# A retention layer and a Strassen feed-forward on one core: one pool of eight PSUM banks, q loaded in permuted 1 KB rows, and wider feed-forward sums

## The chip, the core and the metric

The kernel runs on one core of a Trainium2 chip. A core has TensorE (PE, the matrix multiplications), VectorE (DVE), ScalarE (ACT), GpSimd (POOL) and SyncE (SP), which here issues transfers; each engine runs its own list of instructions in order, and semaphores hold an instruction until those on other engines that it depends on are done. DMA engines move data between HBM and SBUF; PSUM holds the results of TensorE in banks of 2 KB for each of 128 partitions, here 512 numbers of fp32. The metric is the time of one execution on the device in microseconds (us), the median of several.

## What is computed

Eight sequences of 576 positions with eight heads of width 64 go through a retention layer (attention without softmax, with a decay for each head), and the result through a feed-forward layer with a squared ReLU:

```python
scores = (q @ k.transpose(0, 1, 3, 2)) / sqrt(64)
gamma  = 1.0 - 2.0 ** (-5.0 - arange(8))            # one for each head
ret    = scores * where(i >= j, gamma ** (i - j), 0)
attn   = ret @ v                                    # [8, 8, 576, 64]
x      = attn.transpose(0, 2, 1, 3).reshape(4608, 512)
h      = x @ w_in                                   # 512 -> 2048
out    = maximum(h, 0) ** 2 @ w_out                 # 2048 -> 512
```

Inputs and output are fp32; the kernel multiplies in fp16 and accumulates in fp32.

## The kernel before

**Units and groups.** A unit is 128 positions: 32 "full" units (a stretch of 128 positions of one sequence) and 4 "tail" units (the last 64 positions of two sequences). Two units form a group, 18 in all. The first eight units are "paired" and take another path, with their transposes on TensorE; the other 28 are what most of the change touches.

**Retention of a group.** k, q and v of a unit are loaded by SyncE (`add_load`, L284), cast to fp16 by POOL (L359, `fk` and `fq` in `add_unit`) and, for v, scaled with the decay (L371, `fv`). A DMA transpose (L384) gives kqT, heads and positions turned round. All multiplications of the retention are done by `quad` (L345): four matmuls of 64x64 side by side on TensorE's array. They come in four kinds: scores psc (`emit_scores`, L602), which DVE masks into rT (L682, `after_scores`); state sums psS (`emit_sums`, L613), which DVE turns into the running states Rm, stmp and R (`after_sums`); the share of the earlier state, "out1" (L648), and the rest, "out2" (L653), which add up in psO. DVE scales psO with the decay into xT (L736, `after_outs`), the left side of the feed-forward.

**Joined clusters.** For groups g from 7 to 16 the quads of two groups are joined (`add_ret`, L751): f1 is out1 of g and the scores of g+1; f2 is the sums of g+1 and out2 of g. Each is one unbroken stretch on TensorE. f2 needs the masked scores and the casts of both groups.

**Feed-forward of a group** (`add_ff`, L836). Eight blocks: 8 matmuls of 128x256 into one PSUM bank ph (L859), a ReLU on ACT (L867) into rl, and a square into gT, on ACT (L877) for seven blocks and on DVE (L879) for one (five of eight on DVE in the last two groups). The second product, from group 2 on, is a 2x2 Strassen scheme in Winograd's form (`add_strassen`, L915): seven products p1 to p7 of 8 matmuls each (L951), whose left sides are either parts of gT or four sums of parts, S1 to S4, made by DVE (L928, tile gS), and whose right sides are parts of w_out or differences of them, wT (L811). DVE makes each of the four sums in two halves of 512 columns, eight operations per group. Products collect in banks po, copied out by ACT (L964) and added by DVE (L974) into the output tile o.

**PSUM.** Four single banks (tag `ff`) rotate between ph, po and a few others. The retention has two pairs of banks: `prS` for psc, `prO` for psO; psS takes one of the two. A pair comes free as a whole.

**The order.** `Schedule` (L16 to L93) is a list planner that runs while the program is built: each task has an engine, a key (lower is preferred), a length, tasks that it follows and resources with counts (`ff=4`, `prS=1`, `prO=1`, `rT=4`, ...). It runs the tasks through an event model and writes them out in the order in which they start there; the engines then run that order as it stands, whatever the true times are. A length or a count changed in the planner can therefore move instructions of every engine. In a joined cluster of the kernel before, TensorE's order is: 40 matmuls of ph, 16 of po, 12 ph, 4 po, 4 ph, 12 po, 4 ph, 8 po; then f1 (16 groups of out1 quads, 32 of scores); 4 ph, 16 po; then f2 (32 of sums, 48 of out2).

Of the kernel before, what the change touches and what calls it, by code (L numbers as in the profile page):

```python
# [103 lines left out]
def kernel(  # L104
# [48 lines left out]
    ps_ff = ctx.enter_context(tc.tile_pool(name="ps_ff", bufs=4, space=bass.MemoryType.PSUM))  # L153
    ps_ret = ctx.enter_context(tc.tile_pool(name="ps_ret", bufs=1, space=bass.MemoryType.PSUM))
# [42 lines left out]
    heads = [(4 * n + 2 * a + b, n, a, b) for n in range(2) for a in range(2) for b in range(2)]  # L197
    lncol = const.tile([P, NP], FP32, name="lncol")
    lnrow_R = const.tile([P, NP], FP32, name="lnrow_R")
    for h, n, a, b in heads:  # L200
        nc.vector.memset(lncol[64 * b:64 * b + 64, 2 * n + a:2 * n + a + 1], lng[h])
        nc.vector.memset(lnrow_R[64 * a:64 * a + 64, 2 * n + b:2 * n + b + 1], lng[h])

    mask = const.tile([P, 64], FP32, name="mask")
    nc.gpsimd.memset(mask, 1.0)
    for c in range(2):
        nc.gpsimd.affine_select(out=mask[c * 64:(c + 1) * 64], in_=mask[c * 64:(c + 1) * 64],  # L207
                                compare_op=ALU.is_ge, fill=0.0, base=0, pattern=[[1, 64]], channel_multiplier=-1)
# [9 lines left out]
    for hp in range(NP):  # L218
        nc.scalar.activation(out=gam_f[:, hp, :], in_=iota_f, func=ACTF.Exp, scale=lncol[:, hp:hp + 1])
    gam = {"full": gam_f.rearrange("p n (c i) -> p c n i", c=2),  # L220
           "tail": gam_f[:, :, 0:64].rearrange("p n (c i) -> p c n i", c=1).to_broadcast([P, 2, NP, 64])}
# [7 lines left out]
    SPREAD = 0.1  # L229
    SQ_LATE = (1, 4, 6)  # L230
# [4 lines left out]
    SHARED = ()  # L235
    FIRST = ["k0", "q0", "v0", "k2", "q2", "v2", "w0", "w1", "w2", "w3", "w4", "w5", "w6", "w7", "k4", "q4", "v4", "k6", "q6", "v6"]
    sched = Schedule(dict(ff=4, prS=1, prO=1, g=3, ld=5, wst=4, kq=7, v16=7, rT=4, x=3, rl=3, o=4, p1=2, u2=2, u4=2,
# [6 lines left out]
    warm_ps = []  # L244

# [17 lines left out]
    def make_tail_pool():  # L263
        iota_pt = tile_of["iota_pt"] = const.tile([P, 1], FP32, name="iota_pt")
        nc.gpsimd.tensor_copy(out=iota_pt[0:64], in_=iota_p[0:64])
        nc.gpsimd.tensor_scalar(out=iota_pt[64:128], in0=iota_p[64:128], scalar1=-64.0, scalar2=None, op0=ALU.add)
    tail_pool = add_gated("POOL", 4, "v", 2.2, make_tail_pool)
# [14 lines left out]
    def add_load(u):  # L282
        kind, b, c = units[u]
        for n, (name, src) in enumerate((("k", k), ("q", q), ("v", v))):  # L284
            def fn(name=name, src=src):
                x = ld.tile([P, H, D], FP32, name=f"{name}32", tag=f"{name}32")
                tile_of[name + "32", u] = x
                if kind == "full":
                    nc.sync.dma_start(out=x, in_=src[b, :, c * P:(c + 1) * P, :].rearrange("h p d -> p h d"))
                else:  # L290
                    for i in range(2):
                        nc.sync.dma_start(out=x[i * 64:(i + 1) * 64],
                                          in_=src[b + i, :, 512:576, :].rearrange("h p d -> p h d"))
            loaded[name, u] = dma_task(0, 1.2 if loaded else 2.1, fn, acq=("ld",) if n == 0 else ())
# [58 lines left out]
    def add_unit(u, base):  # L353
# [4 lines left out]
        def sorted_cast(op, out_, in_):  # L358
            op(out=out_.rearrange("p (n b a d) -> p n b a d", n=2, b=2, a=2),  # L359
               in_=in_.rearrange("p (n a b) d -> p n b a d", n=2, a=2))  # L360
# [5 lines left out]
        def fq():  # L366
            sorted_cast(nc.gpsimd.tensor_copy, tile_of["kq", u][:, 1], tile_of["q32", u])
# [19 lines left out]
    def add_unit_pair(u, base):  # L387
# [4 lines left out]
        for i, name in enumerate("kqv"):  # L392
            xs[name] = []
            for e in range(2):
# [3 lines left out]
                def fc(name=name, e=e, eng=eng):  # L398
# [8 lines left out]
                    else:  # L407
                        engines[eng](out=t.rearrange("p (n b a d) -> p n b a d", n=2, b=2, a=2),
                                     in_=x.rearrange("p (n a b) d -> p n b a d", n=2, a=2))
# [42 lines left out]
    def add_ret_pair(g):  # L452
# [7 lines left out]
        for e in range(2):  # L460
            tag = "prS" if e == 0 else "prO"

            def fs(e=e, tag=tag):
                ps = rT["ps", e] = ps_ret.tile([P, 2, 512], FP32, name="psc", tag=tag)
                rT[e] = cast.tile([P, 2, NP, P], FP16, name="rx", tag="kq16")
                for hp in range(NP):
                    for a, s in ((0, 0), (1, 1), (0, 1), (1, 0)):
                        quad(ps[half(s), a, hp * P:(hp + 1) * P], kqT(s)[half(a), hp, half(e)], kqT(s)[half(a), NP + hp, :],
                             a, s)
            t = add("PE", base + 3 + e, 0.4, fs, deps=T["kqT", u] + T["kqT", u + 1], acq=(tag, "kq"))  # L470
            ms = []
            for a in range(2):
                def fm(e=e, a=a):
                    nc.vector.tensor_tensor(
                        out=rT[e][:, a], in0=rT["ps", e][:, a].rearrange("p (n i) -> p n i", i=P),
                        in1=mask2[:, e].rearrange("p (o e) i -> p o (e i)", o=1).to_broadcast([P, NP, P]), op=ALU.mult)
                def fc(e=e):
                    nc.scalar.copy(out=rT[e][:, 1], in_=rT["ps", e][:, 1].rearrange("p (n i) -> p n i", i=P))

                def fp(e=e):  # L480
                    nc.gpsimd.tensor_tensor(
                        out=rT[e][:, 1], in0=rT[e][:, 1],
                        in1=mask2[:, e].rearrange("p (o e) i -> p o (e i)", o=1).to_broadcast([P, NP, P]), op=ALU.mult)
                if a and g in SHARED:
                    c = add("ACT", -60 + e, 0.66, fc, deps=[t])
                    reads = ms + [c]
                    ms.append(add("POOL", -60 + e, 0.75, fp, deps=[c]))
                else:
                    ms.append(add("DVE", base + 5 + e, 0.66, fm, deps=[t] + ms))
                    reads = ms  # L490
            sched.free(tag, reads)
            masked += ms

        def fk():
            ps = rT["sum"] = [ps_ff.tile([P, 512], FP32, name="psS", tag="ff") for s in range(2)]
            for hp in range(NP):
                for e in range(2):
                    for s, a in ((0, 0), (1, 1), (0, 1), (1, 0)):
                        h = 4 * (hp // 2) + 2 * a + hp % 2
# [32 lines left out]
        def inter(other):  # L532
            for n in range(2):
                for a, b in ((0, 0), (1, 1), (0, 1), (1, 0)):
                    s = a ^ other
                    if s or carry:
                        x = 2 * n + b
                        put2(s, 4 * n + 2 * a + b, before(s)[half(a), half(x)], kqT(s)[half(a), NP + x, :], a)

        def put2(s, h, lhsT, rhs, row):  # L540
            col = h % 2
            quad(tile_of["psO", g][half(col), s, 128 * (h // 2):128 * (h // 2) + 128], lhsT, rhs, row, col,
# [3 lines left out]
        def fo1():  # L546

            tile_of["psO", g] = ps_ret.tile([P, 2, 512], FP32, name="psO", tag="prO")
            for m in range(NP):
                for e in range(2):  # L550
                    for s, b in ((0, 0), (1, 1), (0, 1), (1, 0)):
                        h = 2 * m + b
                        put2(s, h, tile_of["vx", u][half(s), e, 64 * h:64 * h + 64],
                             rT[e][half(s), m % 2, 2 * (m // 2) + b, :], s)
# [5 lines left out]
        t = add("PE", base + 23.9, 0.6, fo1, deps=masked + T["kvx", u], acq=("prO",))  # L560
# [8 lines left out]
        for s in range(2):  # L569
            def fx(s=s):  # L570
                if s == 0:
# [3 lines left out]
                    in0=tile_of["psO", g][:, s].rearrange("p (n e i) -> p n e i", n=NP, e=2),  # L575
                    in1=gam_f.rearrange("p n (i e) -> p n e i", e=2), op=ALU.mult)
            T["x", u + s] = add("DVE", base + 25 + s, 0.7, fx, deps=[t] + ([T["x", u]] if s else []), acq=() if s else ("x",))
        sched.free("prO", [T["x", u + 1]])
# [22 lines left out]

    def emit_scores(g):  # L602

        tile_of["psc", g] = ps_ret.tile([P, 2, 512], FP32, name="psc", tag="prS")
        for s, u in enumerate(units_of(g)):
            kT = tile_of["kqT", u]
            ps = tile_of["psc", g][:, :, cols(s)].rearrange("p a (n i) -> p a n i", i=64)
            for hp in range(NP):
                for a, c in ((0, 0), (1, 1), (0, 1), (1, 0)):
                    quad(ps[half(c), a, hp, :], kT[half(a), hp, half(c)], kT[half(a), NP + hp, half(c)], a, c)  # L610

    def emit_sums(g, tag):
# [3 lines left out]
        tile_of["psS", g] = ps_ret.tile([P, 2, 512], FP32, name="psS", tag=tag)  # L616
        for s, u in enumerate(units_of(g)):
            if u not in full_of(g):
                continue
            ps = tile_of["psS", g][:, :, cols(s)].rearrange("p c (n i) -> p c n i", i=64)  # L620
            for hp in range(NP):
                for c, a in ((0, 0), (1, 1), (0, 1), (1, 0)):
                    h = 4 * (hp // 2) + 2 * a + hp % 2
                    quad(ps[half(a), c, hp, :], tile_of["kq", u][half(c), 0, half(2 * hp + a)],
# [6 lines left out]
    def put(g, u, c, h, lhsT, rhs, row):  # L631
        col = h % 2
        s = units_of(g).index(u)
        quad(tile_of["psO", g][half(col), c, 256 * s + 64 * (h // 2):256 * s + 64 * (h // 2) + 64], lhsT, rhs, row, col,
# [3 lines left out]
    def inter(g, u, other):  # L638
        st = states(u)
        for n in range(2):  # L640
            for a, b in ((0, 0), (1, 1), (0, 1), (1, 0)):
                c = a ^ other
                if c in st:
                    x = 2 * n + b
                    put(g, u, c, 4 * n + 2 * a + b, tile_of[st[c][:2]][half(a), st[c][2], half(x)],
                        tile_of["kqT", u][half(a), NP + x, half(c)], a)

    def emit_out1(g):  # L648
        tile_of["psO", g] = ps_ret.tile([P, 2, 512], FP32, name="psO", tag="prO")
# [3 lines left out]
    def emit_out2(g):  # L653
        for u in units_of(g):
            for m in range(NP):
                for c, b in ((0, 0), (1, 1), (0, 1), (1, 0)):
                    h = 2 * m + b
                    put(g, u, c, h, tile_of["v16", u][half(c), h, :],
                        tile_of["rT", u][half(c), m % 2, 2 * (m // 2) + b, :], c)
# [18 lines left out]
    def after_scores(g, t, key):  # L678
        for s, u in enumerate(units_of(g)):
            def fm(s=s, u=u):  # L680
                r = tile_of["rT", u] = work.tile([P, 2, NP, 64], FP16, name="rT", tag="rT")
                tile_of["masking", g] = nc.vector.tensor_tensor(  # L682
                    out=r, in0=tile_of["psc", g][:, :, cols(s)].rearrange("p a (n i) -> p a n i", i=64),
                    in1=mask.rearrange("p (o r i) -> p o r i", o=1, r=1).to_broadcast([P, 2, NP, 64]), op=ALU.mult)
            m = add("DVE", key + s, 0.7, fm, deps=[t] + (T["masked", g][-1:] if s else []), acq=("rT",))
# [3 lines left out]
    def after_sums(g, t, key, res):  # L689
# [5 lines left out]
        def fr0():  # L695
            r = tile_of["Rm", g] = st_pool.tile([P, 2, NP * D], FP16, name="Rm", tag="Rm", bufs=2)
            x = tile_of["psS", g][:, 0]
# [5 lines left out]
        def fr1():  # L703
            r = tile_of["tmp", g] = work.tile([P, 2, NP * D], FP32, name="stmp", tag="stmp", bufs=1)
            nc.vector.tensor_tensor(out=flat(r), in0=tile_of["psS", g][:, 1], in1=flat(tile_of["Rm", g]), op=ALU.add)
# [9 lines left out]
        T["Rm", g], T["R", g], T["Rread", g], T["Rmread", g] = r0, r2, [], r1  # L715
        sched.free(res, [r1])

    def after_outs(g, t1, t2, key):
        us = units_of(g)
        n = len(us)  # L720
        for u in us:
            sched.free("kqT", [t2])
            sched.free("v16", [t2])
            sched.free("rT", [t2])
            for name, rg, at in states(u).values():
                if name == "R":
                    T["Rread", rg].append(t2)
                elif at == 0:
                    sched.free("Rm", [t2, T["Rmread", rg]])
        for u in us:  # L730
            s, at = groups[g].index(u), us.index(u)

            def fx(s=s, at=at, u=u):
                if ("x", g) not in tile_of:
                    tile_of["x", g] = x_pool.tile([P, NP, n * P], FP16, name="xT", tag="xT")
                nc.vector.tensor_tensor(  # L736
                    out=tile_of["x", g][:, :, s * P:(s + 1) * P].rearrange("p n (c i) -> p c n i", c=2),
                    in0=tile_of["psO", g][:, :, cols(at)].rearrange("p c (n i) -> p c n i", i=64),
                    in1=gam[units[u][0]], op=ALU.mult)
# [351 lines left out]
```

## Time and profile before

The time before is 290.57 us (median of 3 runs, 290.51 to 290.76); the profiled execution spans 289.1 us, at the full TensorE clock.

| what | value |
|---|---|
| TensorE, DVE, ACT, POOL busy | 282.1, 182.4, 188.2, 84.1 us |
| share of the chain of waits on TensorE | 91% |
| matmul ph (L859), 1152 of them | 139.9 us busy |
| squares and sums of DVE (L879, L928), 154 of 512 columns | 76.5 us busy |
| masks rT (L682), xT (L736), 28 each | 683, 684 ns each |
| ReLU and square on ACT for one block | 588 + 631 ns |
| POOL casts of k and of q (L359), v scaling (L371) | 663, 660, 1057 ns each |
| POOL idle until k, until q, until v has landed | 60.2, 30.6, 20.9 us |
| transfers on the input queue | 75.3% of 16 DMA engines over the span |
| q loads: from issue to landing, median | 5.1 us |

The profile gives busy time per engine, the chain of waits (the work that ended last, followed back to what released each step), groups of like instructions with the mean time of one and the idle time before them, and a timeline. A line "L928 ... gS<-gT,gS 128x512 f16<-128x512 f16 x64 | 32.8, 517 | 14.2" reads: line 928, output gS from inputs gT and gS, shape and types of output and input, 64 such instructions, 32.8 us busy in all, 517 ns each, and 14.2 us for which the engine sat idle before them. In a timeline the first two columns are start and duration in us; a square bracket holds the idle time before and what ended it. TensorE's matmuls overlap in its pipeline, so their pace is read from their starts and not from their durations.

### The profile page before, as it was taken

How to read it: one execution, taken by the hardware profiler on the slowest of the kernel's cores; microseconds unless marked ns; L12 is line 12 of the kernel's file. 1: busy time of each engine (PE TensorE's matmuls, PEld its weight loads, DVE VectorE, ACT ScalarE, POOL GpSimd, SP SyncE). 2: the span in 40 equal slices, each digit the busy share in tenths (PEclk: the TensorE clock that was granted, in tenths of full speed). 3: DMA queues.
4: the chain of work that ended last, by engine and by line, in shares of the span. 5: the costliest groups of instructions: out<-in, count | busy, mean ns of one | idle time of the engine just before them, and what ended most of it. 6: DMA issues, size and time to landing. Idle time of an engine off the chain costs nothing.

```text
span 289.1 us, 9988 instructions
## 1 busy us (share of the span) xinstructions
PE 282.1 (98%) x4322; PEld 234.3 (81%) x4322; DVE 182.4 (63%) x381; ACT 188.2 (65%) x361; POOL 84.1 (29%) x121
## 2 busy tenths in 40 slices
PE   8999999999999999999999999999999999999994
PEld 3568755788888888888888888888888888888883
DVE  3772368769585657736686857575777775455622
ACT  5459964685757676767756767676767676747830
POOL 5660035443333243342506061505250500000000
PEclk9999999999999999999999999999999999999999
DMA  7999999999999689999788799899995920201004
GB/s 202 274 208 206 249 291 267 219 203 202 221 188 198 153 201 199 217 219 219 154 199 168 172 194 205 163 196 206 225 182 151 181 76 2 75 2 73 2 8 139
DMA packets 139436, 49.94 MB, mean 173 GB/s; under 512 B 118144, under 2 KB 135040, under 8 KB 139392
## 3 DMA queue, kind: packets, MB, share of 16 engines
q1 hardware_dynamic: 134848, 44.84, 75.3%
q0 software_dynamic: 4224, 4.19, 8.8%
q8 instruction: 34, 0.56, 0.8%
q10 hardware_dynamic: 320, 0.26, 0.4%
q14 instruction: 10, 0.08, 0.1%
HBM read 36.70 MB, written 9.44 MB: 160 GB/s over the span
## 4 chain that ended last, share of the span: by engine, by line
PE 91%; DMA 3%; issue 2%; POOL 2%; DVE 0%; POOLq 0%; DVEq 0%
PE ph L859 44%; PE po L951 34%; PE po L899 5%; PE psO L345 4%; DMA w_in<-in_moe_w_in_dram 3%; PE psc L345 2%; PE psS L345 2%; PE psT L423 1%; POOL mask L215 0%; POOL vx L404 0%; POOL w_in L319 0%; DVE o L974 0%; POOL mask L207 0%; DVE p L1003 0%; POOL mask L211 0%
## 5 line engine op out<-in xcount | busy, mean ns | idle before, releaser
L859 PE MATMUL ph<-xT,w_in 128*128 128x256 f16 x1152 | 139.9, 273 | 0.1
L859 PEld LDWEIGHTS <-w_in 128*128 128x128 f16 x1152 | 110.9, 98 | 14.8 <-DMA w_in<-in_moe_w_in_dram 0.3
L867 ACT ACTIVATE rl<-ph 128x512 f16<-128x512 f32 x144 | 84.5, 588 | 52.5 <-PE ph L859 50.9
L877 ACT ACTIVATE gT<-rl 128x512 f16<-128x512 f16 x118 | 74.4, 631 | 3.4
L951 PEld LDWEIGHTS <-gS 128*128 128x128 f16 x512 | 49.8, 98 | 5.9
L951 PE MATMUL po<-wT,gS 128*128 128x256 f16 x384 | 52.1, 273 | 0.0
L928 DVE TENSOR_TENSOR gS<-gT,gS 128x512 f16<-128x512 f16 x64 | 32.8, 517 | 14.2 <-ACT gT L877 13.5
L951 PEld LDWEIGHTS <-gT 128*128 128x128 f16 x384 | 37.1, 98 | 4.5
L928 DVE TENSOR_TENSOR gS<-gT 128x512 f16<-128x512 f16 x64 | 30.9, 485 | 12.6 <-ACT gT L877 12.5
L359 POOL CAST kq<-k 128x512 f16<-128x512 f32 x28 | 18.6, 663 | 61.4 <-DMA k<-in_k_dram 60.2
L951 PE MATMUL po<-w_out,gT 128*128 128x256 f16 x256 | 34.7, 273 | 0.0
L371 POOL TENSOR_TENSOR v<-v,vdec_full 128x512 f16<-128x512 f32 x24 | 25.4, 1057 | 21.9 <-DMA v<-in_v_dram 20.9
L359 POOL CAST kq<-q 128x512 f16<-128x512 f32 x28 | 18.5, 660 | 30.8 <-DMA q<-in_q_dram 30.6
L964 ACT COPY u<-po 128x256 f32<-128x256 f32 x32 | 11.8, 369 | 19.1 <-PE po L951 18.9
L974 DVE TENSOR_TENSOR o<-po,u 128x256 f32<-128x256 f32 x31 | 13.0, 420 | 16.3 <-PE po L951 10.0
L736 DVE TENSOR_TENSOR xT<-psO,gam_full 128x512 f16<-128x512 f32 x28 | 18.1, 684 | 6.3 <-PE psO L345 6.2
L682 DVE TENSOR_TENSOR rT<-psc,mask 128x512 f16<-128x512 f32 x28 | 18.3, 683 | 4.6 <-PE psc L345 4.5
L879 DVE TENSOR_TENSOR gT<-rl 128x512 f16<-128x512 f16 x26 | 12.8, 492 | 12.6 <-ACT rl L867 11.9
L974 DVE TENSOR_TENSOR o<-po,p 128x256 f32<-128x256 f32 x17 | 7.2, 423 | 17.8 <-ACT u L964 8.8
L951 PE MATMUL po<-wT,gT 128*128 128x256 f16 x128 | 16.8, 273 | 0.0
L951 PE MATMUL po<-w_out,gS 128*128 128x256 f16 x128 | 16.8, 273 | 0.0
L899 PE MATMUL po<-w_out,gT 128*128 128x512 f16 x64 | 15.7, 380 | 0.0
(78 smaller groups left out, 224.0 us busy)
## 6 DMA issues: line engine op xcount, KB each, us to landing
out_dram<-o SPq DMA_DIRECT2D x32, 256.0 KB, 3.7
k<-in_k_dram SPq DMA_DIRECT2D x24, 256.0 KB, 4.8
q<-in_q_dram SPq DMA_DIRECT2D x24, 256.0 KB, 5.1
v<-in_v_dram SPq DMA_DIRECT2D x24, 256.0 KB, 4.9
pair<-in_k_dram SPq DMA_DIRECT2D x4, 512.0 KB, 7.0
pair<-in_q_dram SPq DMA_DIRECT2D x4, 512.0 KB, 7.2
pair<-in_v_dram SPq DMA_DIRECT2D x4, 512.0 KB, 7.0
w_in<-in_moe_w_in_dram POOLq DMA_DIRECT2D x4, 512.0 KB, 8.9
```

The costliest lines, as they stand in the source:

```text
L345: t = nc.tensor.matmul(out_, lhsT=lhsT, rhs=rhs, start=start, stop=True, skip_group_check=True, tile_position=(64 * row, 64 * col))
L359: op(out=out_.rearrange("p (n b a d) -> p n b a d", n=2, b=2, a=2), in_=in_.rearrange("p (n a b) d -> p n b a d", n=2, a=2))
L371: nc.gpsimd.tensor_tensor(out=t, in0=tile_of["v32", u], in1=vdec[kind].rearrange("p (h o) -> p h o", o=1).to_broadcast([P, H, D]), op=ALU. ...
L682: tile_of["masking", g] = nc.vector.tensor_tensor(out=r, in0=tile_of["psc", g][:, :, cols(s)].rearrange("p a (n i) -> p a n i", i=64), in1 ...
L736: nc.vector.tensor_tensor(out=tile_of["x", g][:, :, s * P:(s + 1) * P].rearrange("p n (c i) -> p c n i", c=2), in0=tile_of["psO", g][:, :, ...
L859: nc.tensor.matmul(tile_of["ph", g, fb][:, j, :], lhsT=w_in16[:, m, fi * P:(fi + 1) * P], rhs=tile_of["x", g][:, m, :], start=(m == 0), st ...
L867: nc.scalar.activation(out=t, in_=tile_of["ph", g, fb], func=ACTF.Relu)
L877: nc.scalar.activation(out=t, in_=rl, func=ACTF.Square)
L899: nc.tensor.matmul(tile_of["po", u], lhsT=tile_of["g", g][:, fi, s * P:(s + 1) * P], rhs=w_out16[:, fi, :], start=(fi == 0), stop=(fi == N ...
L928: nc.vector.tensor_tensor(out=Sx(k, h), in0=in0(h), in1=in1(h), op=op)
L951: nc.tensor.matmul(tile_of["pb", g, bank], lhsT=left(i), rhs=right[:, i, :], start=(start and i == 0), stop=(i == HF - 1), skip_group_chec ...
L974: nc.vector.tensor_tensor(out=o_tile(u)[:, half * HM:(half + 1) * HM], in0=bank(x), in1=tile_of[name, g], op=ALU.add)
```

## The change

It has four parts.

1. **One pool of PSUM banks.** All eight banks are in `ff`. `banks(name)` gives two of them to psc, psS, psO or the paired groups' sums; a task takes `"ff","ff"` in the planner in addition to `prS` or `prO`. Each bank goes back when its own reader is done. So that a reader frees a bank, masks, and the scaling into xT, run per bank instead of per unit: two of each for a group, as before. rT is one tile for a group.
2. **q in permuted rows.** Each full unit's q (units from 8 on) comes by four transfers whose rows are 1 KB, four consecutive positions of one head, instead of one transfer with rows of 256 B. The cast on POOL puts the data in place with a permuted access pattern; what stays permuted (positions in the order 4r+t) is undone where kqT is read, as the moving operand of scores and out1/out2, in four runs of 16 columns, by a mask with the pattern [[1, 4], [4, 16]] and by reading psO with a stride when xT is made. The order of heads changes with it (h = 4a + 2n + b instead of 4n + 2a + b). There are two masks in fp16 now, one for full units and one for tails, each with one memset and two selects on POOL at the start.
3. **Wider sums.** S1, S3 and S4 are one operation of 1024 columns each; S2 stays in two halves. The planner counts 0.8 for a whole sum, and 0.5 and 0.9 for the halves of S2 (0.55 for each half before).
4. **A pause.** f2 of a joined cluster becomes ready in the planner 1.5 us after its inputs (`lag=PAUSE`), which moves it behind other work. A q load counts 0.8 instead of 1.2 us on SyncE.

In a joined cluster the order written for TensorE becomes: 40 matmuls of ph, 16 of po; f1; 4 ph, 4 po, 8 ph, 4 po, 4 ph, 16 po, 8 ph, 16 po; f2. The number of matmuls of each kind is the same.

```diff
-    ps_ff = ctx.enter_context(tc.tile_pool(name="ps_ff", bufs=4, space=bass.MemoryType.PSUM))
-    ps_ret = ctx.enter_context(tc.tile_pool(name="ps_ret", bufs=1, space=bass.MemoryType.PSUM))
+    ps_ff = ctx.enter_context(tc.tile_pool(name="ps_ff", bufs=8, space=bass.MemoryType.PSUM))
...
-    mask = const.tile([P, 64], FP32, name="mask")
-    nc.gpsimd.memset(mask, 1.0)
...
+    mask = {}
+    for kind, pattern in (("tail", [[1, 64]]), ("full", [[1, 4], [4, 16]])):
+        m = mask[kind] = const.tile([P, 64], FP16, name=f"mask_{kind}")
+        nc.gpsimd.memset(m, 1.0)
+        for c in range(2):
+            nc.gpsimd.affine_select(out=m[c * 64:(c + 1) * 64], in_=m[c * 64:(c + 1) * 64],
+                                    compare_op=ALU.is_ge, fill=0.0, base=0, pattern=pattern, channel_multiplier=-1)
...
+    QL = 0.8
+    BESIDE = 0.9
+    PAUSE = 1.5
+    PARTS = 1
...
-    sched = Schedule(dict(ff=4, prS=1, prO=1, g=3, ld=5, wst=4, kq=7, v16=7, rT=4, x=3, rl=3, o=4, p1=2, u2=2, u4=2,
+    sched = Schedule(dict(ff=8, prS=1, prO=1, g=3, ld=5, wst=4, kq=7, v16=7, rT=2, x=3, rl=3, o=4, p1=2, u2=2, u4=2,
...
+    def banks(name):
+        return [ps_ff.tile([P, 512], FP32, name=name, tag="ff") for i in range(2)]
...
+                if kind == "full" and name == "q":
+                    for j in range(NP):
+                        nc.sync.dma_start(out=x[32 * j:32 * j + 32].rearrange("r (a t) d -> r a (t d)", a=2),
+                                          in_=src[b, :, c * P:(c + 1) * P, :].rearrange("(a x) (r t) d -> x r a (t d)", a=2, t=4)[j])
...
+                nc.gpsimd.tensor_copy(out=tile_of["kq", u][:, 1].rearrange("p (t a d) -> p a t d", t=4, a=2),
+                                      in_=tile_of["q32", u].rearrange("p (a t) d -> p a t d", a=2))
...
+    def qT(u, a, x, c):
...
-        for s, u in enumerate(units_of(g)):
-            def fm(s=s, u=u):
-                r = tile_of["rT", u] = work.tile([P, 2, NP, 64], FP16, name="rT", tag="rT")
+        for a in range(2):
+            def fm(a=a):
+                if a == 0:
+                    tile_of["rT", g] = work.tile([P, 2, 2, NP, 64], FP16, name="rT", tag="rT", bufs=2)
...
+                    out=tile_of["rT", g][:, :, a],
+                    in0=tile_of["psc", g][a].rearrange("p (s n i) -> p s n i", s=2, i=64),
...
+            sched.free("ff", [m])
...
+                    in0=y.rearrange("p (o t r) -> p o r t", o=n * NP, t=4) if full else y.rearrange("p (o r t) -> p o r t", o=n * NP, t=4),
...
-                     acq=("prO", "prS"))
+                     acq=("prO", "prS", "ff", "ff", "ff", "ff"))
...
-                     deps=[t1] + T["masked", g] + T["masked", g + 1] + sums_deps(g + 1), acq=("prS",) if full_of(g + 1) else ())
+                     deps=[t1] + T["masked", g] + T["masked", g + 1] + sums_deps(g + 1), acq=("prS", "ff", "ff") if full_of(g + 1) else (), lag=PAUSE)
...
-            for h in range(2):
-                def f(h=h):
+            for h in range(parts):
+                def f(sl=cut(parts, h)):
...
-                out_.append(add("DVE", key + h, 0.55, f, deps=deps(h)))
+                out_.append(add("DVE", key + h, (BESIDE if h else 0.5) if parts > 1 else 0.8, f, deps=deps(h, parts) + list(start)))
...
-        s3 = add_sum(2, base - 12, lambda h: G(0, 0, h), lambda h: G(1, 0, h), ALU.subtract, low)
+        s3 = add_sum(2, base - 12, PARTS, G(0, 0), G(1, 0), ALU.subtract, part(0))
...
+        s2 = add_sum(1, base - 4 - early, 2, G(1, 1), S_(2), ALU.subtract, lambda h, parts: part(1)(h, 2) + [of(s3, h)])
+        s1 = add_sum(0, base + 1 - early, PARTS, G(1, 0), G(1, 1), ALU.add, lambda h, parts: part(0)(h, parts) + part(1)(h, parts) + s3[:1])
+        s4 = add_sum(3, base + 4 - early, PARTS, G(0, 1), S_(1), ALU.subtract, lambda h, parts: s2 if parts == 1 else [s2[h]])
```

## The prediction

> **What bounds the kernel now.** I read the engine totals first, then the chain of waits, then what TensorE waited for.
>
> ```profile
> PE 282.1 (98%) x4322; PEld 234.3 (81%) x4322; DVE 182.4 (63%) x381; ACT 188.2 (65%) x361; POOL 84.1 (29%) x121
> ...
> PE 91%; DMA 3%; issue 2%; POOL 2%; DVE 0%; POOLq 0%; DVEq 0%
> ```
> ```profile
> PE warm L249 <- DVE wT L164: 1.3, 1, 1.3
> PE psS L345 <- POOL vx L404: 0.5, 1, 0.5
> ```
>
> TensorE is busy for 98% of the span, is 91% of the chain, and after the warm-up waits once, for 0.5 us. A busy TensorE can still run below its pace, so I counted starts in its timeline: dense matmuls of 256 columns start every 109.3 ns from about 20 us to 284 us, and each change between them and the small quad matmuls loses 0.104 us. The quad stretches repeat: f1 takes 0.51 us, f2 0.76 to 0.78. Three are longer than their kind: 0.91 (at 160.4 us), 0.83 (188.5) and 0.77 against 0.64 (106.7). That is 0.13 + 0.07 + 0.12 = **0.32 us** of stall in the whole stream. No other engine's saved work shortens anything; only a new or a removed TensorE wait counts.
>
> DVE, by groups and then in one joined cluster's timeline:
>
> ```profile
> L928 DVE TENSOR_TENSOR gS<-gT,gS 128x512 f16<-128x512 f16 x64 | 32.8, 517 | 14.2 <-ACT gT L877 13.5
> ...
> L682 DVE TENSOR_TENSOR rT<-psc,mask 128x512 f16<-128x512 f32 x28 | 18.3, 683 | 4.6 <-PE psc L345 4.5
> ```
> ```profile
> 209.72 1.09 DVE L879 TENSOR_TENSOR gT<-rl 128x512 f16<-128x512 f16 x1
> 210.84 0.72 DVE L928 TENSOR_TENSOR gS<-gT,gS 128x512 f16<-128x512 f16 x1
> 211.48 0.41 DVE L928 TENSOR_TENSOR gS<-gT 128x512 f16<-128x512 f16 x1
> 211.82 0.82 DVE L928 TENSOR_TENSOR gS<-gT,gS 128x512 f16<-128x512 f16 x1
> ```
>
> The same operation takes 0.42 us or up to 1.3. Of the 154 sums and squares on DVE, 27 took over 0.55 us, 12.1 us above 0.42 in all, 0.45 each; all 27 lay beside a POOL operation. These are POOL's beside the four above:
>
> ```profile
> 209.49 1.04 POOL L371 TENSOR_TENSOR v<-v,vdec_full 128x512 f16<-128x512 f32 x1 [0.17 <-POOL kq L359]
> 210.59 0.69 POOL L359 CAST kq<-k 128x512 f16<-128x512 f32 x1
> 211.70 0.67 POOL L359 CAST kq<-q 128x512 f16<-128x512 f32 x1 [0.42 <-DMA q<-in_q_dram]
> ```
>
> **What the Trainium skill says.** "SBUF — State Buffer", section "Who interferes with whom": a DVE instruction with two SBUF inputs and a GpSimd instruction that reads SBUF exclude each other, and the later one is held back. The trace agrees: 1.09 us against 0.42 beside POOL, while masks rT, which read PSUM and one SBUF operand, stay at 672 to 693 ns. The same page, section "Door 1", has 16-byte lines in SBUF and 8-byte lines in PSUM, with a penalty for crossing lines; no run here shows a strided read of that kind. "DMA: Bandwidth & Descriptors", section "Why small descriptors are slow (HBM only)": packets under 512 B waste the engine; here 256 B took 22.7 ns and 512 B 32.2, so bytes per time rise by 1.4.
>
> **The change part by part.**
>
> *q in 1 KB rows.* A unit's q was 1024 packets of 256 B, 1024 x 22.7 / 16 = 1.45 us of the 16 DMA engines; it becomes 256 of 1 KB, between half of that and (with 94.8 ns, the price of the casting weight rows of 1 KB) 256 x 94.8 / 16 = 1.52 us. For 24 units 0 to 17 us are saved. TensorE waits for no load, so this is worth nothing; it brings POOL's q casts (30.6 us idle for q) earlier. SyncE issues 3 more per unit, 72 x 0.43 to 0.84 us = 31 to 60 us of 289; loads, transposes and stores queue behind them, with time to spare.
>
> *Permuted q as moving operand.* Four rows of 16 fp16, 32 bytes a run, for scores and inter products: about 768 quads, 192 rounds of four. At 26.7 ns a round, unharmed 0, rate halved 192 x 26.7 = 5.1 us. A 32-byte run fills two lines whole, so I take **0** and keep 5.1 for the range.
>
> *xT and masks.* Two xT and two masks per group remain. xT now reads PSUM in strides: 684 ns, at worst about twice the streaming part, 1.22 us. Then xT is done 1.07 us later. In steady clusters the first matmul that reads it follows it by 4.7 us, so that is hidden; only one early group has 0.39 us, costing 0.7. I take 0. Mask per bank reads the same number of elements: 0.68 as now.
>
> *Three sums as one.* 48 pairs become single operations. The price is in this kernel, the weight differences of 1024 columns:
>
> ```profile
> L811 DVE TENSOR_TENSOR wT<-w_out x4: 683/684/693, 28.5 to 36.8; 128x1024 f16<-128x1024 f16 x4
> ```
>
> A pair takes 0.34 + 0.42 = 0.76, so DVE saves 48 x 0.08 = 3.8 us. DVE is no bound: worth 0 directly. The first half of a sum is available 0.3 us later, but products start well after.
>
> *Eight shared banks and PAUSE.* The order written by the schedule keeps all matmuls and all 39 quad stretches, but in steady clusters f1 (out1 and the next scores) comes 44 matmuls earlier and f2 is 64 matmuls behind f1 instead of 20. This gives f2's inputs 7 us instead of 2.2, so the 0.32 us should mostly go. The new item: psc is now two of the banks that rotate for ph and po, so a feed-forward product waits for the **masks rT** to release a bank. In seven clusters this is product 2's bank (po), in six a block of ph, some clusters having both; before, none waited on a mask. Behind it on TensorE stands everything.
>
> Worked in the cluster above. f2 ends at 203.42; 40 ph + 16 po are 56 x 0.1093 = 6.12, f1 starts at 209.54, ends at 210.05. 24 matmuls later, 2.62 us, at 212.67, product 2 wants its bank. DVE: ReLU of the last block ends at 209.69, its square runs 209.72 to 210.14, second half of S2 from 210.17, S1 from 210.51, S4 from 211.11 (0.60 apart as one operation), first mask 211.71 to **212.39**. Slack 0.28 us, with no POOL beside it. With the excess that this cluster showed (1.09 - 0.42, 0.72 - 0.42, 0.82 - 0.42 = 1.37 us) the stall is 1.37 - 0.28 = **1.1 us**.
>
> POOL's times shift with the loads, so I take the mean: 27 of 154 is 0.175 per operation, 0.45 each. The four, two of them double length, count as about five: none hit 0.38 (stall 0), one 0.40 (0.45 - 0.28 = 0.17), two or more 0.21 (0.62 to 1.1, say 0.7). Mean 0.07 + 0.15 = 0.22 us. Some nine clusters have such a wait, so 9 x 0.22 = **2.0 us**. A square or S2 half beside v scaling gives the large ones.
>
> *Start and end.* Three more POOL operations before the weights (one memset, two selects; about 0.65 us) fall in 4.05 us in which POOL is idle before it issues w_in. The last groups keep their order: 0.
>
> Sum: +2.0 - 0.3 = +1.7, so 290.57 + 1.7 = about **292.2**.
>
> **Rivals.** *Hidden:* POOL's operations, earlier with q, miss the squares and sums, and the slack of 0.28 holds. For it: rT alone takes its time undisturbed, and 0.38 of clusters have no hit. Against it: POOL works in all clusters. Only 0.3 is won: **290.3**, no measurable change. *Stacked:* the strided q reads slow quads (up to 5.1 us), or most clusters stall like the one worked out (9 x 1.1 = 9.9, half of that 5): about **295.0**. Against: the line rule of 32 bytes, and the spread of hits. *Faster:* the stalls go, and with four more banks part of the 0.104 us at each of the some 78 changes goes too, 8.1 us in all; a tenth of it and 0.3 give 1.1: **289.5**. Against: the loss is the same at every change, whatever bank is next, so it does not look like a bank wait.
>
> **How the numbers follow.** Forecast 0.46, hidden 0.23, stacked 0.14, faster 0.17. The forecast's case reaches from +0.4 (slack a little larger, two stalls) to +3.5; I take 291.2 to 294. Slower by over 0.2% (above 291.15): nearly all of 0.46 plus 0.14 = 0.60; within: 0.23; faster (below 289.99): 0.17. The range, 289.9 to 294.6, leaves out the outer parts of stacked and faster, a fifth in all.
>
> **What would show it.** Step by step: TensorE waits on DVE rT at po (L951) and ph (L859), 0.2 to 1 us each, 2 us in sum; f2 stretches all at 0.76 to 0.78 with 0.32 us gone; f1's quads still at 0.51 us (if longer, strided reads cost); xT at 0.68 (or up to 1.2); single sums at 0.69, with some at 1.1 or more beside POOL; 39 quad stretches with the same 0.104. What would make me wrong: no wait on rT at all (slack mis-sized), or a stream denser than 109.3 ns.

## The result and the profile after

The changed kernel takes 292.47 us (median of 4 runs, 292.20 to 292.92) against 290.66 for the kernel before, measured again beside it: a ratio of 1.0062, 95% interval 1.0045 to 1.0079. It is slower by 1.8 us; 292.2 was forecast.

The engine totals and the chain that ended last, from the page of the changed kernel:

```profile
PE 281.4 (97%) x4322; PEld 233.6 (80%) x4322; DVE 176.2 (61%) x333; ACT 187.6 (65%) x361; POOL 89.9 (31%) x124
...
PE 40%; DVE 1%; issue 0%; DVEq 0%
```

DVE lost 6 us of work, TensorE has the same 4322 matmuls, and yet the span grew from 289.1 to 290.5 us. The chain was 91% TensorE before. Now it goes back to 169.65 us and ends there on a DVE mask, with the rest of the span left out: a matmul at 170.30 was released by that mask. What TensorE waited for (total, times, longest):

```profile
PE warm L254 <- DVE wT L163: 1.3, 1, 1.3
PE po L970 <- DVE rT L690: 1.2, 2, 0.9
PE psT L437 <- DVE kx L422: 1.1, 1, 1.1
PE psS L355 <- POOL vx L418: 0.2, 1, 0.2
```

The second line is new and is the one that the prediction named for po; a wait of ph on rT, which it named too, is not there. (The wait of psT lies in the start, before the first ph at 17.74 us, which is where it was before.) This view counts the idle time behind the modelled ends of matmuls; from the starts, as in the prediction, the stalls of the dense stretches are 1.03 us at 66 us, 0.51 at 170 and 0.10 at 185, together 1.64 us. The quad stretches gained about 0.25 us. 1.64 - 0.25 is 1.39, the difference of the spans.

The sums and masks of DVE, as groups:

```profile
L943 DVE TENSOR_TENSOR gS<-gT 128x1024 f16<-128x1024 f16 x32 | 24.5, 764 | 8.2 <-ACT gT L891 8.1
L943 DVE TENSOR_TENSOR gS<-gT,gS 128x512 f16<-128x512 f16 x32 | 17.5, 546 | 10.9 <-ACT gT L891 9.9
L690 DVE TENSOR_TENSOR rT<-psc,mask_full 128x512 f16<-128x512 f32 x24 | 16.2, 680 | 0.0
```

The masks take 680 ns as before; sums of 1024 columns, 0.68 us when nothing disturbs them, average 0.76. The largest stall in three timelines, DVE, POOL and TensorE in this order (start, duration, instruction):

```profile
62.39 0.42 DVE L893 TENSOR_TENSOR gT<-rl 128x512 f16<-128x512 f16 x1 [1.21 <-ACT rl L881]
62.85 0.80 DVE L943 TENSOR_TENSOR gS<-gT,gS 128x512 f16<-128x512 f16 x1
63.57 0.68 DVE L943 TENSOR_TENSOR gS<-gT 128x1024 f16<-128x1024 f16 x1
64.17 1.52 DVE L943 TENSOR_TENSOR gS<-gT,gS 128x1024 f16<-128x1024 f16 x1
65.62 0.68 DVE L690 TENSOR_TENSOR rT<-psc,mask_full 128x512 f16<-128x512 f32 x1
```
```profile
62.76 0.62 POOL L380 CAST kq<-q 128x512 f16<-128x512 f32 x1 [0.31 <-DMA q<-in_q_dram]
63.71 1.44 POOL L385 TENSOR_TENSOR v<-v,vdec_full 128x512 f16<-128x512 f32 x1 [0.33 <-DMA v<-in_v_dram]
65.10 1.07 POOL L369 CAST kq<-k 128x512 f16<-128x512 f32 x1
```
```profile
66.35 1.03 PE L970 MATMUL po<-w_out,gT 128*128 128x256 f16 x8 [0.86 <-DVE rT L690]
```

The second half of S2 met the q cast (0.80 against 0.42), S4 met the scaling of v (1.52 against 0.68): 1.22 us more. The mask behind them ended at 66.30, and product 2 began 0.05 us later. POOL pays as well: its scaling of v takes 1.44 and a cast 1.07, against 1.04 and 0.61 alone.

A steady cluster without a stall, the same three views:

```profile
211.10 0.43 DVE L893 TENSOR_TENSOR gT<-rl 128x512 f16<-128x512 f16 x1 [1.21 <-ACT rl L881]
211.56 0.42 DVE L943 TENSOR_TENSOR gS<-gT,gS 128x512 f16<-128x512 f16 x1
211.90 0.69 DVE L943 TENSOR_TENSOR gS<-gT 128x1024 f16<-128x1024 f16 x1
212.50 0.69 DVE L943 TENSOR_TENSOR gS<-gT,gS 128x1024 f16<-128x1024 f16 x1
213.10 0.68 DVE L690 TENSOR_TENSOR rT<-psc,mask_full 128x512 f16<-128x512 f32 x1
```
```profile
209.58 1.21 POOL L385 TENSOR_TENSOR v<-v,vdec_full 128x512 f16<-128x512 f32 x1
```
```profile
214.15 1.04 PE L970 MATMUL po<-w_out,gT 128*128 128x256 f16 x8
```

POOL is done 0.31 us ahead of the square; the mask ends at 213.79, 0.36 us before product 2 wants its bank.

### The profile page after: what moved, and what is told of

It reads as the page before. It is cut to its first block, busy times and chain, and to the rows that moved or that the text cites. A ratio compares the mean times of both kernels' runs of the same rounds, so it can differ in the third digit from the quotient of the medians.

```text
span 290.5 us, 10071 instructions
## 1 busy us (share of the span) xinstructions
PE 281.4 (97%) x4322; PEld 233.6 (80%) x4322; DVE 176.2 (61%) x333; ACT 187.6 (65%) x361; POOL 89.9 (31%) x124
## 3 DMA queue, kind: packets, MB, share of 16 engines
q1 hardware_dynamic: 117568, 44.84, 69.1%
## 5 line engine op out<-in xcount | busy, mean ns | idle before, releaser
L943 DVE TENSOR_TENSOR gS<-gT,gS 128x512 f16<-128x512 f16 (+1 forms) x48 | 31.7, 661 | 10.9 <-ACT gT L891 9.9
L369 POOL CAST kq<-k 128x512 f16<-128x512 f32 x28 | 21.1, 754 | 50.1 <-DMA k<-in_k_dram 46.9
L385 POOL TENSOR_TENSOR v<-v,vdec_full 128x512 f16<-128x512 f32 x24 | 26.3, 1097 | 25.0 <-DMA v<-in_v_dram 23.0
L943 DVE TENSOR_TENSOR gS<-gT 128x1024 f16<-128x1024 f16 x32 | 24.5, 764 | 8.2 <-ACT gT L891 8.1
L380 POOL CAST kq<-q 128x512 f16<-128x512 f32 x24 | 17.1, 714 | 26.0 <-DMA q<-in_q_dram 25.7
L893 DVE TENSOR_TENSOR gT<-rl 128x512 f16<-128x512 f16 x26 | 11.3, 436 | 22.1 <-ACT rl L881 22.1
L690 DVE TENSOR_TENSOR rT<-psc,mask_full 128x512 f16<-128x512 f32 x24 | 16.2, 680 | 0.0
```

What stands on the lines that cost most here:

```text
L380: nc.gpsimd.tensor_copy(out=tile_of["kq", u][:, 1].rearrange("p (t a d) -> p a t d", t=4, a=2), in_=tile_of["q32", u].rearrange("p (a t) d ...
L385: nc.gpsimd.tensor_tensor(out=t, in0=tile_of["v32", u], in1=vdec[kind].rearrange("p (h o) -> p h o", o=1).to_broadcast([P, H, D]), op=ALU. ...
L690: tile_of["masking", g] = nc.vector.tensor_tensor(out=tile_of["rT", g][:, :, a], in0=tile_of["psc", g][a].rearrange("p (s n i) -> p s n i" ...
L943: nc.vector.tensor_tensor(out=tile_of["S", g][:, k, sl], in0=in0(sl), in1=in1(sl), op=op)
```

## The experiments

**Theory A** is the prediction's: a product waits for a PSUM bank that a mask frees, and the mask is late because it stands on DVE behind a square and sums that POOL holds up. **Theory B**: the permuted q costs the time. **Theory C**: sums of 1024 columns come too late. **Rival D**: the longer way from f1 to f2. Each ratio is to the kernel before, run on the same chip. Where a sum or square is called lengthened, it took over 0.12 us more than undisturbed (0.42 us for 512 columns, 0.68 for 1024).

| run | median us | ratio, 95% interval |
|---|---|---|
| changed kernel | 292.47 | 1.0062 (1.0045 to 1.0079) |
| masks first | 290.88 | 1.0009 (1.0001 to 1.0017) |
| pools apart | 290.86 | 1.0006 (0.9998 to 1.0014) |
| POOL reads little | 290.91 | 1.0011 (1.0003 to 1.0019) |
| v scaled twice | 294.14 | 1.0115 (1.0095 to 1.0135) |
| sums in halves | 292.85 | 1.0077 (1.0064 to 1.0090) |
| no pause | 292.69 | 1.0068 (1.0056 to 1.0081) |
| q as before | 292.44 | 1.0059 (1.0047 to 1.0071) |
| before, wide sums | 290.83 | 1.0005 (0.9997 to 1.0013) |
| POOL shifted | 291.95 | 1.0042 (1.0029 to 1.0054) |
| masks first, S3 in halves | 290.60 | 0.9998 (0.9990 to 1.0007) |

**Masks first.** The order as planned, with 11 masks moved on DVE only ("sum" marks S1 and S4):

```diff
+        for m in [t for t in order if "first_mask" in t]:
+            i, f = order.index(m), order.index(m["first_mask"])
+            late = [t for t in order[f + 1:i] if "sum" in t]
...
+            order[f + 1:i + 1] = [t for t in order[f + 1:i] if t not in late] + [m] + late
         for t in order:
             t["fn"]()
```

> The changed kernel with one thing moved: in each group the first mask rT stands on DVE ahead of the sums S1 and S4, 11 masks in all; every other engine keeps its order, and banks, loads and sums are as in the changed kernel. Theory A (a product waits for its PSUM bank, which the mask frees too late because it stands behind sums that POOL holds up): the waits of po on rT go, the mask ends about 1.3 us earlier in a steady cluster, and the time is 290.3 to 290.8 us, about 1.8 less than the 292.47 of the changed kernel. Theory B (the permuted q, its 96 transfers or its strided reads cost the time): 292.2 to 292.9, as the changed kernel. Theory C (sums of 1024 columns are finished too late for their own products): slower than the changed kernel, since S1 and S4 come 0.6 us later still.

290.88 us, just above the range expected: 1.6 us of the 1.8 are back with nothing changed but the place of 11 DVE instructions; TensorE, ACT and POOL run the same instructions in the same order. DVE's sums and squares are lengthened by 10.0 us in all, as much as in the changed kernel, so it is not their length by itself that costs. The cluster of the largest stall, DVE's timeline of this run:

```profile
62.89 0.72 DVE L950 TENSOR_TENSOR gS<-gT,gS 128x512 f16<-128x512 f16 x1
63.53 0.68 DVE L695 TENSOR_TENSOR rT<-psc,mask_full 128x512 f16<-128x512 f32 x1
64.13 1.43 DVE L950 TENSOR_TENSOR gS<-gT 128x1024 f16<-128x1024 f16 x1
65.48 0.68 DVE L950 TENSOR_TENSOR gS<-gT,gS 128x1024 f16<-128x1024 f16 x1
```

S1 is held up just the same, to 1.43 us, but nobody waits for it: the mask was done at 64.21. Theories B and C fall as the main cause. One stall of 0.23 us is left, at 164.84, where product 7 waited for an S3 of 1.53 us beside POOL.

**Pools apart.**

```diff
-    ps_ff = ctx.enter_context(tc.tile_pool(name="ps_ff", bufs=8, space=bass.MemoryType.PSUM))
+    ps_ff = ctx.enter_context(tc.tile_pool(name="ps_ff", bufs=4, space=bass.MemoryType.PSUM))
+    ps_ret = ctx.enter_context(tc.tile_pool(name="ps_ret", bufs=2, space=bass.MemoryType.PSUM))
...
-                     acq=("prO", "prS", "ff", "ff", "ff", "ff"))
+                     acq=("prO", "prS"))
```

> The changed kernel with part one undone: four banks for the feed-forward and two pairs for the retention again, everything else (q rows, wide sums, the pause) kept; TensorE's order stays nearly the same. Theory A: no product can wait on a mask, so 290.2 to 290.7 us, at or a little below the kernel before. Theory B or C: 292.2 to 292.9.

290.86 us, 0.2 above the range expected. The stretches are nearly those of the changed kernel, f2 64 matmuls behind f1 in the steady clusters, so it was not the eight banks that moved f1. The dense stretches from 20 us on have no stall, though DVE's sums and squares are lengthened by 9.5 us. Its profile is of the slowest of 13 runs (291.99) and has one f2 stretch of 1.83 us at 131 us, with no wait that the profile names.

**POOL reads little.**

```diff
-            sorted_cast(nc.gpsimd.tensor_copy, t[:, 0], tile_of["k32", u])
+            nc.gpsimd.memset(t[:, 0, D:], 0.1)
+            nc.gpsimd.tensor_copy(out=t[:, 0, 0:D], in_=tile_of["k32", u][:, 0, :])
...                                                        # q and v in the same way
```

> The changed kernel, where POOL's casts of k and q and its scaling of v (units from 8 on) read only 64 of 512 columns and fill the rest with a constant by a memset, which reads no SBUF: seven of eight heads are left out. All orders of TensorE, DVE, ACT and SyncE are kept. Theory A with the contention as its cause: squares and sums stay at 0.42 and 0.69 us, the uncontended slack of 0.28 us holds, and the time is 290.3 to 290.8 us. Theory A without contention (the masks are late by their place alone), or theory B: 292.2 to 292.9.

290.91 us, 0.1 above the range expected, and no dense stretch from 20 us on has a stall. Groups of this run, by DVE and POOL:

```profile
L942 DVE TENSOR_TENSOR gS<-gT 128x1024 f16<-128x1024 f16 x32 | 22.2, 694 | 8.2 <-ACT gT L890 8.1
L942 DVE TENSOR_TENSOR gS<-gT,gS 128x512 f16<-128x512 f16 x32 | 13.6, 425 | 12.5 <-ACT gT L890 11.8
```
```profile
L374 POOL MEMSET kq<- 128x448 f16 x28 | 13.2, 470 | 0.0
```

None of the 106 sums and squares is lengthened (the longest takes 0.78 us for 1024 columns); in the changed kernel 20 are, by 10.0 us in all, every one beside a POOL operation. DVE's order is the same in both, and POOL is busy for 79.8 us here against 89.9. So it is POOL's reading that makes the masks late, and their place alone is harmless. The Trainium skill, "SBUF — State Buffer", section "Who interferes with whom", limits the conflict to GpSimd operations that read SBUF. POOL's 84 memsets of 0.47 us here agree: 21 sums and squares ran beside one of them, and none was lengthened.

**v scaled twice.**

```diff
-            nc.gpsimd.tensor_tensor(
-                out=t, in0=tile_of["v32", u],
+            for i in range(2):
+                nc.gpsimd.tensor_tensor(
+                    out=t, in0=tile_of["v32", u],
...
```

> The changed kernel with the scaling of v on POOL done twice over (28 more POOL operations of about 1.05 us, 29 us on an engine that is 31% busy), all other orders kept. Theory A: sums and squares are hit more often, POOL's time beside them rises by a third, and the stalls of 1.6 us grow: 293.2 to 296 us. Theory B or C: POOL's later v has time to spare, 292.2 to 292.9.

294.14 us, 1.7 more. What TensorE waited for in this run:

```profile
PE po L971 <- DVE rT L691: 1.6, 1, 1.6
...
PE po L971 <- DVE gS L944: 0.7, 1, 0.7
...
PE ph L874 <- DVE rT L691: 0.3, 1, 0.3
```

More work on an engine that is 31% busy lengthens the kernel, through DVE. From the starts its stalls sum to 3.3 us. 2.3 of them are waits for masks; in 0.8 at 168 us a product waits for a sum of 1024 columns that POOL had held up to 1.53 us.

**Sums in halves, order kept.**

```diff
...
-                    nc.vector.tensor_tensor(out=tile_of["S", g][:, k, sl], in0=in0(sl), in1=in1(sl), op=op)
+                    for sl in [cut(2, h)] if parts > 1 else [cut(2, 0), cut(2, 1)]:
+                        nc.vector.tensor_tensor(out=tile_of["S", g][:, k, sl], in0=in0(sl), in1=in1(sl), op=op)
```

> The changed kernel with S1, S3 and S4 as two operations of 512 columns again, written one after the other in the place of the single one, so that every engine keeps its order. Theory A (banks wait for masks behind the sums): each pair takes 0.76 us instead of 0.68, two pairs stand before the mask, the slack of a steady cluster falls from 0.28 to 0.12 us: 292.6 to 294 us, a little slower than the changed kernel. Theory C (a single operation of 1024 columns is what makes the masks or the products late): 290.4 to 291.2.

292.85 us, not below the changed kernel: the wide sums do not cost the time. Whether they save a little in front of a mask can't be told from the times, whose intervals overlap.

**No pause.**

```diff
-    PAUSE = 1.5
+    PAUSE = 0.0
```

> The changed kernel with PAUSE at 0: f2 stands some 12 matmuls earlier in the joined clusters, f1, the masks and the sums where they were. Theory A: the waits of po on rT stay, 291.9 to 293 us. Rival D (the distance from f1 to f2, which holds psO's banks longer, costs the time): 290.4 to 291.2.

292.69 us. The edit did less than I expected: f2 comes 12 to 20 matmuls earlier in three joined clusters up to 160 us and stays where it was in all later ones, and the largest stall lies ahead of all joined clusters. So this run says little on D; the wait of po on rT is there again (0.8 us). What rules D out as the cause are masks first and pools apart: f2 is as far behind f1 there, and the time is back.

**q as before.**

```diff
-                if kind == "full" and name == "q":
-                    for j in range(NP):
-                        nc.sync.dma_start(...)
-                elif kind == "full":
+                if kind == "full":
...
-        return t[:, x, half(c)] if units[u][0] == "tail" else t[:, :, 32 * x + 16 * c:32 * x + 16 * c + 16]
+        return t[:, x, half(c)]
```

> The changed kernel with part two undone: q of a unit in one transfer with rows of 256 B, the cast, the moving operand, the mask and the reading of psO without the permutation; TensorE, DVE and ACT keep their order. Theory A: the waits stay, only which of POOL's operations they meet changes, 291.6 to 293.2 us. Theory B (the permuted q is the cost): 290.3 to 290.9. If the strided read of q slowed the quads, f1's stretch of 0.51 us would be shorter here; I expect 0.51 again.

The cast, the mask and the reading of psO are put back in the same way. 292.44 us, f1 at 0.51 and xT at 684 ns in both. Theory B is out.

**The kernel before with wide sums alone.**

```diff
-            for h in range(2):
+            for h in range(2 if k == 1 else 1):
...
-                out_.append(add("DVE", key + h, 0.55, f, deps=deps(h)))
+                out_.append(add("DVE", key + h, 0.55 if k == 1 else 0.8, f, deps=deps(h) if k == 1 else deps(0) + deps(1)))
```

> The kernel before with part three alone: S1, S3 and S4 as single operations of 1024 columns, planned at 0.8 us, four and four banks as before. Theory A: nothing on TensorE waits for a mask or a sum, so 290.3 to 290.9 us, as before. Theory C: 291.5 or more.

290.83 us, no change that can be told from none, with the sums and squares lengthened by 9.1 us. C is out as the cause of the changed kernel's loss. In other orders a product did wait for a whole S3, as in masks first.

**POOL shifted.**

```diff
+            for i in range(2):
+                nc.gpsimd.memset(t, 0.0)
             nc.gpsimd.tensor_tensor(
                 out=t, in0=tile_of["v32", u],
```

> The changed kernel with two memsets of the v tile ahead of each scaling of v on POOL; they read no SBUF, and where the scaling directly follows a cast they push it back by about 1 us. Orders of TensorE, DVE and ACT are kept, no work beside DVE's sums is added. In the profile of the changed kernel the steady clusters from 197 us on have no stall, because the scaling of v ends 0.3 us before the square (209.58 + 1.21 = 210.79 against 211.10). Theory A1 (hits are fixed by the phase of POOL against DVE, the same in cluster after cluster): the scaling now lies beside the square, costs it some 0.5 us, 0.2 us more than the slack, in each of the steady clusters, and the early stalls move: 292.9 to 295 us, with waits of po on rT after 197 us. Theory A2 (hits fall by chance): 292.2 to 293, no stall in one cluster after the other.

291.95 us, below both ranges: a miss, and it leaves the question open. In the steady clusters the memsets ran while POOL would have waited for v, and the scaling came earlier (208.18 us) instead of later, so the meeting that I wanted to force didn't occur. What did move is the earlier stalls: 0.19 in place of 1.03 at 65 us, 0.46 in place of none at 95, 0.27 in place of 0.51 at 170, and a wait for S3 of 0.23 at 166.

**Masks first, S3 in halves.**

```diff
...
+                    for sl in [cut(2, 0), cut(2, 1)] if k == 2 else [cut(parts, h)]:
```

> The changed kernel with the first masks ahead of S1 and S4, as in the run with masks first (290.88 us), and S3 in two halves again: there the one stall left, 0.24 us at 164.8 us, was product 7 waiting for a whole S3 of 1.53 us beside POOL. Theory A: that stall goes, and with f2's 0.3 us of the kernel before gone too the time is 290.4 to 290.8, at best 0.1% below the kernel before. If something else than the masks still cost time, it stays at 290.9 or more.

290.60 us against 290.77 for the kernel before; the interval takes in 1. No dense stretch from 20 us on has a stall. The changed kernel's loss is undone, and nothing beyond it can be told from none: with TensorE's pace and its 39 quad stretches as they are, some 0.3 us were there to win.

## Why the prediction was right

**The bound and the mechanism.** Right, as worked out from the kernel before: a product's wait on the mask, product 2 first of all, behind square, S2, S1 and S4. Without POOL, from the square's start to the mask's end, 2.67 us were predicted (209.72 to 212.39); the steady cluster above took 2.69. The blocks of ph that were to wait on a mask too did not wait in the changed kernel; they did in v scaled twice (0.48 us at 83 us) and sums in halves (0.22 at 82). The slack was put at 0.28 us. Excess of the four operations over their undisturbed times, less the stall that followed, gives it directly:

| kernel, mask at | excess | stall | slack |
|---|---|---|---|
| changed, 66 us | 1.23 | 1.03 | 0.20 |
| changed, 170 us | 0.83 | 0.51 | 0.32 |
| changed, 185 us | 0.42 | 0.10 | 0.32 |
| v scaled twice, 67 us | 2.00 | 1.81 | 0.19 |
| q as before, 170 us | 0.71 | 0.40 | 0.31 |
| sums in halves, 171 us | 0.91 | 0.72 | 0.19 |

In these places the slack lies between 0.19 and 0.32 us, and what goes beyond it is stall. Other clusters have more room: at 156 us in the changed kernel an excess of 1.24 us stalled nothing, at 95 us with POOL shifted 0.94 stalled 0.46, and where TensorE had just stalled for another reason (170 us with POOL shifted) 0.83 stalled 0.27.

**The sum of the stalls.** 2.0 us were predicted, 1.64 are in the profile: near, but in part by luck. Nine clusters were each to lose 0.22 us on average. In the changed kernel 11 clusters have a mask behind sums; six of them had one of the four operations lengthened, close to the share assumed (0.62), but three of the six had the room to take it, and the other three lost 0.55 on average. That POOL works in all clusters, the argument against the rival "hidden", was wrong as well. POOL's busy share in the changed kernel, from its page:

```profile
POOL 5660035334425234162625343351615000000000
```

Each digit is a fortieth of the span, busy in tenths. POOL's last operation ends at 224.92 us, so the clusters at 228 and 243 us had nothing to meet. And the hits go with places. In the changed kernel and the five variants that keep shared banks, masks behind the sums and POOL's reading, the clusters at about 65, 80, 155 and 170 us are hit every time, those at 155 without a stall, and the clusters from 212 us on have an excess of at most 0.02 us and no stall. A chance of 0.175 for each operation is therefore no model of it. Why these places, when POOL follows its loads, was to be tested with POOL shifted, and stays open for the others. The size of a hit (0.45 predicted) was 0.50.

**The gain.** 0.32 us of stall in the quads was to go, and about 0.25 went. The three long stretches gave back 0.29 us: f2 is at 0.76 to 0.78 throughout, and the 0.77 of 106.7 us is 0.67 (it is no f2, so the distance from f1 can't be its reason). One at 47 us gave another 0.10. But the other scores with sums (0.64 before) take 0.67 now and once 0.75, 0.15 more together.

**Edits costed at nothing.** q: no cost on TensorE, 292.44 without it. The input queue's share fell from 75.3% of 289.1 to 69.1% of 290.5 us, 17 us less for each DMA engine. Not all of it is q's own: 6144 packets of 1 KB took 64 ns each where 24576 of 256 B had taken 22.7 (the mean of all packets of that size), an estimated 10 us for each engine; packets of the other loads got shorter too. From issue to landing:

```profile
q<-in_q_dram SPq DMA_DIRECT2D x24, 256.0 KB, 5.1
q<-in_q_dram SPq DMA_DIRECT2D x96, 64.0 KB, 3.4
```

The second line, of the changed kernel, is for one of four transfers. A whole unit, from the first issue to the last landing, took 4.9 us (median), so a whole q landed hardly faster. Reads of q at half rate were put at 5.1 us for the range; a round of four quad matmuls mostly takes 32 ns in the trace, so 6.1 would have been due. xT with a stride: 684 ns, as before. Sums: 0.68 to 0.69; DVE's busy time fell by 6.2 us where 3.8 were predicted, about 2 of it because fewer hits came. That products start well after their sums holds in the changed kernel, but not in every order: with masks first, one waited 0.23 us for a whole S3. The start: first ph at 17.74 us in both.

**What the median has more.** The profiled executions differ by 292.27 - 290.92 = 1.35 us, the medians by 1.8: the profile shows one of the shorter executions of the changed kernel, whose runs spread over 0.7 us, and one of the longer ones of the kernel before. Where the longer ones lose more is not in a trace here. Nor is it shown why masks first, pools apart and POOL reads little, without the stalls, are not below the kernel before by the 0.25 us or so that their quad stretches should gain.

The rivals: "hidden" needed POOL to miss the sums, and the run where POOL reads little shows that this would have been enough; "stacked" would have needed strided reads that cost, or hits in every cluster; "faster" needed a cheaper change between dense and quad stretches, and that loss is 0.10 us as before.

## What to carry to other kernels

Before buffers of two stages are pooled, ask which engine frees each buffer and what stands ahead of that instruction on its engine: a product that had waited for nothing but ACT and short DVE additions now waited for a mask at the end of a line of sums. Put the instruction that frees a shared buffer ahead of those whose results are wanted later; here moving 11 instructions on one engine gave back 1.6 of 1.8 us. And take the length of such a line under the load of the engines beside it, with the longest durations of the profile and not the medians.

## What the runs showed of the hardware

- The conflict of DVE and POOL costs both: beside each other a sum of 1024 columns took up to 1.5 us against 0.68, the scaling of v 1.44 against 1.04, a cast 1.07 against 0.61. Operations with one SBUF operand and one in PSUM were not lengthened: the 28 masks and the 28 xT of the later groups stayed at 0.67 to 0.69 us in every run, 16 of the masks of the changed kernel beside POOL. (The 672 to 693 ns that the prediction gives for the masks before are the range of xT; the masks took 677 to 692.)
- A memset on POOL doesn't take part: 21 sums and squares beside memsets of 0.47 us, none lengthened.
- After a mask's end, the matmul that waited for it started 0.05 us later.
- A moving operand in four runs of 32 bytes, 16 numbers each, left f1's 48 matmuls at 0.51 us, and reading PSUM with a stride of 64 bytes left a DVE operation of 512 numbers at 684 ns. The penalty for crossing lines that the prediction weighs did not show in either.
